# A sketched attention feeding a feed-forward layer: keys and queries projected as loaded in 64-row tiles, and one written-out task list

## The chip, the cores and the metric

The kernel runs on one core of a Trainium2 chip. The core has five engines, each with its own instruction stream in program order: TensorE (PE in the profile, its weight loads PEld), VectorE (DVE), ScalarE (ACT), GpSimd (POOL) and SyncE (SP, which here only issues DMAs). They wait for each other through semaphores. The metric is the device time of one execution in microseconds, less being better.

## The reference, cut to what matters

```
# q, k, v: (4, 4, 1088, 32) = batch, head, token, dim;  S1, S2: (8, 32)
def phi(x):
    a = einsum('rd,bhsd->bhsr', S1, x)
    b = einsum('rd,bhsd->bhsr', S2, x)
    return einsum('bhsi,bhsj->bhsij', a, b).reshape(..., 64)
q_p, k_p = phi(q), phi(k)
kv  = einsum('bhsf,bhsd->bhfd', k_p, v)
z   = sum(k_p, axis=2)
num = einsum('bhsf,bhfd->bhsd', q_p, kv)
den = einsum('bhsf,bhf->bhs', q_p, z)[..., None] + 1e-06
x   = (num / den).transpose(0, 2, 1, 3).reshape(4352, 128)
h   = x @ w_in                       # w_in: (128, 2048)
out = (h * sigmoid(h)) @ w_out       # w_out: (2048, 128), all inputs and the output float32
```

## The kernel before, in words

The work has two parts: attention, once for each of the four batches, and the feed-forward layer, once for each chunk of tokens. Tokens of a batch are numbered 34 to a partition row when they are loaded (`load_kq`, L89), so a head takes 32 partitions and all four heads fill the 128. `transpose_cols` (L154) turns 32x32 blocks on VectorE, after which partitions hold head and dim and columns hold tokens.

One batch of attention: `project_k` (L203) and `project_q` (L210) multiply the turned keys and queries by S1 and S2 for four heads at a time. The weights WK have 128 rows, and four column tiles of 32 (`tile_position=(0, 32 * c)`) put four groups of tokens on the four partition quarters. `tokens` (L218) turns the result back on VectorE. `outer` (L194) forms the 64 products a_i b_j in bf16, for keys into `kp` and for queries into `qp`. `sum_kv` (L234) multiplies `kp` by V over 18 matmuls. The denominator is bilinear in a and b, so `sum_z` (L221) sums the 8x8 products of the keys, `query_weights` (L227) multiplies them by S2, and `mask_weights` (L230) makes of that a third weight WQb for the queries; `denominators` (L252) finishes it with a product, a reduction and a reciprocal, and `divide` (L259) scales the first query features. `turn` (L263) transposes `qp` on TensorE with an identity, a copy takes it out of PSUM, `numerators` (L274) multiplies by the block-diagonal KVbd, and another copy writes `xT`, the feed-forward's input with dims on partitions.

The feed-forward (`Chunk`, L305; `feed_forward`, L346) takes chunks of 256, 512 and 320 tokens for the first batch and then 512 each, 192 at the end. `hidden` (L317) computes two matmuls of up to 512 columns into one of two PSUM tiles (pool `psH`) and one Silu activation of up to 1024 columns on ScalarE; `output` (L329) accumulates with w_out into one PSUM bank. `store` (L291) writes the turned result with four DMAs or more.

What sets the order: the program order is the schedule (`manual_schedule`, L61). The first batch's attention is written out by hand from L436. The attention of later batches is a generator (L364) that the feed-forward's loop advances by one piece for each step (L509 to L515): batch 1 begins at step 5, batch 2 at step 19, batch 3 at step 35. Loads are ordered by dependencies (L138 to L142): each K or Q of a later batch waits for an earlier load, and V of a later batch, which is cast to bf16 on its way and issued by POOL, waits for the load before it. On POOL these loads are the last instructions.

Of the kernel before, what the change touches and what calls it, by code (L numbers as in the profile page):

```python
# [13 lines left out]
AX = mybir.AxisListType  # L14

# [8 lines left out]
def kernel(  # L24
# [13 lines left out]

    B, H, S, D = q.shape
    R = S1.shape[0]  # L40
    HR = H * R
# [7 lines left out]
    YA = 24  # L49
    assert DM == P and HR == 32 and S == 32 * NY and 3 * NC < NY <= 4 * NC  # L50
# [3 lines left out]
    moeg = ctx.enter_context(tc.tile_pool(name="moeg", bufs=8))  # L54
    outb = ctx.enter_context(tc.tile_pool(name="outb", bufs=2))
    psH = ctx.enter_context(tc.tile_pool(name="psH", bufs=2, space=bass.MemoryType.PSUM))
    psO = ctx.enter_context(tc.tile_pool(name="psO", bufs=1, space=bass.MemoryType.PSUM))
    psP = ctx.enter_context(tc.tile_pool(name="psP", bufs=2, space=bass.MemoryType.PSUM))
    psA = ctx.enter_context(tc.tile_pool(name="psA", bufs=1, space=bass.MemoryType.PSUM))

# [7 lines left out]
    QT = [const.tile([P, 4 * NC * 32], FP32, name=f"QT{i}") for i in range(2)]  # L68
    PQ = [const.tile([P, 3, NC, HR], FP32, name=f"PQ{i}") for i in range(2)]
    AW = [const.tile([P, NC * H, R + 1], FP32, name=f"AW{i}") for i in range(2)]  # L70
    WQb = [const.tile([P, HR], FP32, name=f"WQb{b}") for b in range(B)]
    KVbd = [const.tile([P, 2, 2 * D], BF16, name=f"KVbd{b}") for b in range(B)]
# [3 lines left out]
    xT = const.tile([P, NTOK], BF16, name="xT")  # L76

    S12 = const.tile([R, 2, D], FP32, name="S12")  # L80
# [32 lines left out]

    warm = const.tile([P, 1], FP32, name="warm")
    nc.gpsimd.memset(warm, 0.0)
    ident32 = const.tile([32, 32], FP32, name="ident32")
    make_identity(nc, ident32)
    hmask = const.tile([P, H, R], FP32, name="hmask")
    nc.gpsimd.memset(hmask, 0.0)
    for h in range(H):  # L120
        nc.gpsimd.memset(hmask[D * h: D * (h + 1), h, :], 1.0)
    nc.gpsimd.memset(KT[0][:, NY * 32:], 0.0)
    nc.gpsimd.memset(QT[0][:, NY * 32:], 0.0)
    nc.gpsimd.memset(Vx[96:P, :, NY - 3 * NC: NC, :], 0.0)
    nc.gpsimd.memset(KVbd[0], 0.0)
    for i in range(2):
        nc.gpsimd.memset(AW[i][:, :, R:], 1e-6)
    ident_bf = const.tile([P, P], BF16, name="ident_bf")
    make_identity(nc, ident_bf)
    nc.gpsimd.memset(KT[1][:, NY * 32:], 0.0)  # L130
    nc.gpsimd.memset(QT[1][:, NY * 32:], 0.0)
    for b in range(1, B):
        nc.gpsimd.memset(KVbd[b], 0.0)
# [11 lines left out]
    REP32 = const.tile([32, 4, 32], FP32, name="REP32")  # L145
    nc.vector.tensor_copy(out=REP32, in_=bcast(ident32[:, :], 1, 4))
    rep32 = REP32.rearrange("p h d -> p (h d)")
    REPJ = const.tile([R, 4, R], FP32, name="REPJ")
    nc.vector.tensor_copy(out=REPJ, in_=bcast(ident32[:R, :R], 1, 4))
    hm = const.tile([HR, H], FP32, name="hm")  # L150
    nc.vector.tensor_reduce(out=hm, in_=ident32.rearrange("p (h j) -> p h j", h=H),
                            axis=AX.X, op=ALU.add)

    def transpose_cols(dst, src, b, c0, c1):  # L154
        nc.vector.transpose(out=dst[:, c0:c1],  # L155
                            in_=src[b].rearrange("p a d -> p (a d)")[:, c0:c1])


    st_ps = psA.tile([P, 2 * R], FP32, name="st_ps", tag="acc")
    nc.tensor.transpose(st_ps[:D, 0:R], S12[:, 0, :], ident32[:R, :R])  # L160
    nc.tensor.transpose(st_ps[:D, R:2 * R], S12[:, 1, :], ident32[:R, :R])
    ST_sb = const.tile([D, 2 * R], FP32, name="ST_sb")
    nc.vector.tensor_copy(out=ST_sb, in_=st_ps[:D, :])
    rep_ps = psP.tile([P, 2 * R], FP32, name="rep_ps", tag="proj")
    nc.tensor.matmul(rep_ps, rep32, ST_sb, start=True, stop=True)
    s2_ps = psA.tile([HR, D], FP32, name="s2_ps", tag="acc")
    nc.tensor.matmul(s2_ps, REPJ.rearrange("p h j -> p (h j)"), S12[:, 1, :],
                     start=True, stop=True)
    transpose_cols(KT[0], Kx, 0, 0, 2 * NC * 32)
    WK = const.tile([P, 2, H, R], FP32, name="WK")  # L170
    for i in range(2):
        nc.vector.tensor_tensor(out=WK[:, i], in0=bcast(rep_ps[:, i * R: (i + 1) * R], 1, H),  # L172
                                in1=hmask, op=ALU.mult)
    wk = [WK[:, i].rearrange("p h i -> p (h i)") for i in range(2)]
    transpose_cols(KT[0], Kx, 0, 2 * NC * 32, S)


    L1 = const.tile([HR, H, D], FP32, name="L1")
    nc.vector.tensor_tensor(out=L1, in0=bcast(s2_ps[:, :], 1, H), in1=bcast(hm[:, :], 2, D),
                            op=ALU.mult)  # L180
    l4_ps = psA.tile([P, P], FP32, name="l4_ps", tag="acc")
    L4 = const.tile([P, P], FP32, name="L4")

    def l4():
        nc.tensor.matmul(l4_ps, rep32, L1.rearrange("p h d -> p (h d)"), start=True, stop=True)  # L185
        nc.scalar.activation(out=L4, in_=l4_ps, func=ACT.Copy)  # L186

# [6 lines left out]
    def outer(dst, a, bb):  # L194
        nc.vector.tensor_tensor(  # L195
            out=dst.rearrange("p n h i j -> p (n h) i j"),
            in0=bcast(a.rearrange("p n (h i) -> p (n h) i", h=H), 3, R),
            in1=bcast(bb.rearrange("p n (h j) -> p (n h) j", h=H), 2, R), op=ALU.mult)

    def project_k(ps, kt, n0, n1, weights=wk):  # L203
        for i, w in enumerate(weights):
            for c in range(4):
                nc.tensor.matmul(ps[32 * c: 32 * (c + 1), i, :], w,  # L206
                                 kt[:, (c * NC + n0) * 32: (c * NC + n1) * 32],
                                 start=True, stop=True, tile_position=(0, 32 * c))

    def project_q(ps, weights, qt, n0, n1):  # L210
        q4 = qt.rearrange("p (n c x) -> p n c x", c=4, x=32)
        for i, w in enumerate(weights):
            for c in range(4):
                nc.tensor.matmul(ps[32 * c: 32 * (c + 1), i, :].rearrange(  # L214
                                     "p (n x) -> p n x", x=32), w, q4[:, n0:n1, c, :],
                                 start=True, stop=True, tile_position=(0, 32 * c))

    def tokens(dst, ps):  # L218
        nc.vector.transpose(out=dst, in_=ps.rearrange("p a (n r) -> p a n r", r=32))  # L219

    def sum_z(zacc, pk, n0, n1):  # L221
        for n in range(n0, n1):
            s = n % 4
            nc.tensor.matmul(zacc[32 * s: 32 * (s + 1), :], pk[:, 1, n, :], pk[:, 0, n, :],
                             start=(n < 4), stop=(n + 4 >= NC), tile_position=(0, 32 * s))

    def query_weights(m_ps, zt):  # L227
        nc.tensor.matmul(m_ps, L4, zt, start=True, stop=True)

    def mask_weights(b, m_ps):  # L230
        nc.vector.tensor_tensor(out=WQb[b], in0=m_ps,
                                in1=hmask.rearrange("p h i -> p (h i)"), op=ALU.mult)

    def sum_kv(kv_ps, kp, vb):  # L234
        for p in range(2):
            for n in range(NC):
                nc.tensor.matmul(kv_ps[:, p, :],
                                 kp[:, n, 2 * p: 2 * p + 2].rearrange("p h i j -> p (h i j)"),
                                 vb[:, 2 * p: 2 * p + 2, n, :],
                                 start=(n == 0), stop=(n == NC - 1))  # L240

    def keep_kv(copy, b, kv_ps):
        for i in range(2):
            copy(KVbd[b][64 * i: 64 * (i + 1), :, D * i: D * (i + 1)],
                 kv_ps[64 * i: 64 * (i + 1), :, D * i: D * (i + 1)])
# [300 lines left out]
```

## Time and profile before

| | |
|---|---|
| time, median of 3 runs | 123.84 us (123.51 to 124.39) |
| profiled execution: span from first to last instruction | 122.1 us |
| mean granted TensorE clock in it | 0.983 |
| Silu activations (L325) | 72, 67.7 us busy |
| first-layer matmuls (L322), second-layer matmuls (L335) | 41.5 and 39.3 us busy |
| first Silu starts at | 19.18 us |
| last matmul ends, last output turn (L341) starts | 117.45 us, 117.49 us |

The time is what the runs measure; of the profiled execution the page gives its span, which counts from the first to the last instruction and is the clock of all views. Matmul records overlap, so the sum of their durations is more than the time they take; a chain of waits counts each moment once. In a line of a time line the first number is the start and the second the duration, both in us; the bracket at the end is the idle time before the instruction and what ended it. "x4" means four instructions merged.

### The profile page before, as it was taken

To read this page: it belongs to the slowest core of one execution; us is meant where nothing else is said; L and a number is where in the kernel's file an instruction comes from. 1 tells how busy PE (TensorE), PEld (TensorE's weight loads), DVE (VectorE), ACT (ScalarE), POOL (GpSimd) and SP (SyncE) were. 2 spreads that over 40 slices of the span, in tenths; PEclk is the share of its full clock that TensorE was granted. 3 is DMA by queue.
4 is the path that set the end of the run, shared out by engine and by line. 5 is a ranking of instruction groups with operands and counts; after the bars stand their busy time and mean duration, and the time that the engine had idled before them with its cause. 6 is when DMAs were issued, how large, how long until landed. Compare 5 with 4: busy or idle time off the path is not lost.

```text
span 122.1 us, 2269 instructions
## 1 busy us (share of the span) xinstructions
PE 97.7 (80%) x884; PEld 50.5 (41%) x896; DVE 68.7 (56%) x126; ACT 74.2 (61%) x83; POOL 11.8 (10%) x41
## 2 busy tenths in 40 slices
PE   0397849969999649899982999999838989989940
PEld 0265627644445435435432244445304434434630
DVE  1367693499945996993369649953398430020210
ACT  4005466666576725466981379667843899999920
POOL 6604510701600000000000000000000000000000
PEclk9999999999999999999999599999999999999998
DMA  2799997691994500030013000500031005013151
GB/s 52 263 222 319 182 358 127 195 205 62 222 173 109 87 2 0 2 57 0 3 21 65 0 0 5 86 0 5 0 59 27 0 0 86 0 21 53 17 94 27
DMA packets 24314, 9.80 MB, mean 80 GB/s; under 512 B 21104, under 2 KB 22896, under 8 KB 24304
## 3 DMA queue, kind: packets, MB, share of 16 engines
q1 hardware_dynamic: 20352, 8.03, 26.0%
q0 software_dynamic: 3792, 1.36, 9.8%
q10 hardware_dynamic: 160, 0.26, 0.6%
q8 instruction: 7, 0.11, 0.4%
q14 instruction: 3, 0.02, 0.1%
HBM read 8.78 MB, written 2.23 MB: 90 GB/s over the span
## 4 chain that ended last, share of the span: by engine, by line
PE 59%; DVE 22%; ACT 7%; DMA 5%; issue 4%; SPq 0%; DVEq 0%; ACTq 0%
PE h_ps L322 20%; PE o_ps L335 17%; DVE qp L195 7%; ACT g L325 5%; PE qpt_ps L268 4%; PE pq_ps L214 3%; PE num_ps L277 3%; PE pk_ps L206 3%; DMA Kx<-in_k_dram 3%; DVE o_tt L341 3%; PE h_ps L206 2%; DVE PQ L219 2%; DVE qpt L189 2%; DVE den L256 2%; DVE AW L254 2%
## 5 line engine op out<-in xcount | busy, mean ns | idle before, releaser
L325 ACT ACTIVATE g<-h_ps 128x1024 bf16<-128x1024 f32 (+2 forms) x72 | 67.7, 980 | 31.1 <-PE h_ps L322 25.5
L322 PE MATMUL h_ps<-xT,w_in_bf 128*128 128x512 bf16 (+3 forms) x151 | 41.5, 365 | 1.9 <-ACT g L325 1.4
L335 PE MATMUL o_ps<-g,w_out_bf 128*128 128x512 bf16 (+3 forms) x157 | 39.3, 349 | 0.5
L335 PEld LDWEIGHTS <-w_out_bf 128*128 128x128 bf16 x160 | 15.5, 98 | 14.8 <-issue 1.1
L322 PEld LDWEIGHTS <-w_in_bf 128*128 128x128 bf16 x160 | 13.1, 103 | 15.9 <-issue 11.1
L341 DVE STREAM_TRANSPOSE o_tt<-o_ps 128x512 f32<-128x512 f32 (+3 forms) x10 | 6.3, 631 | 20.6 <-PE o_ps L335 18.8
L268 PE MATMUL qpt_ps<-ident_bf,qp 128*128 128x128 bf16 (+1 forms) x72 | 6.7, 235 | 9.2 <-DVE qp L195 8.5
L195 DVE TENSOR_TENSOR kp<-pk 128x1280 bf16<-128x1280 f32 (+1 forms) x8 | 10.8, 1352 | 0.2
L195 DVE TENSOR_TENSOR qp<-aqs,PQ 128x1024 bf16<-128x1024 f32 (+3 forms) x9 | 10.8, 1223 | 0.2
L268 PEld LDWEIGHTS <-qp 128*128 128x128 bf16 (+1 forms) x72 | 5.0, 106 | 12.8 <-DVE qp L195 10.0
L189 DVE COPY qpt<-qpt_ps 128x1024 bf16<-128x1024 bf16 (+2 forms) x11 | 5.9, 540 | 5.7 <-PE qpt_ps L268 5.7
L189 DVE CAST xT<-num_ps 128x512 bf16<-128x512 f32 (+2 forms) x11 | 5.8, 531 | 4.8 <-PE num_ps L277 4.8
L83 POOL DMA_DIRECT2D Vb<-in_v_dram x12 | 6.5, 548 | 15.1 <-DMA Qx<-in_q_dram 12.3
L155 DVE STREAM_TRANSPOSE KT<-Kx 128x1088 f32<-128x1088 f32 (+2 forms) x5 | 5.4, 1075 | 2.1 <-DMA Kx<-in_k_dram 2.1
L277 PE MATMUL num_ps<-qpt,KVbd 128*64 128x512 bf16 (+3 forms) x24 | 4.7, 383 | 2.2 <-DVE qpt L189 1.4
L155 DVE STREAM_TRANSPOSE QT<-Qx 128x512 f32<-128x512 f32 (+3 forms) x8 | 5.7, 718 | 0.0
L277 PEld LDWEIGHTS <-KVbd 128*64 128x64 bf16 x24 | 1.9, 111 | 7.0 <-issue 6.9
L214 PE MATMUL pq_ps<-QT,WK 128*32 128x128 f32 (+2 forms) x112 | 4.7, 284 | 0.0
L206 PE MATMUL h_ps<-KT,WK 128*32 128x160 f32 (+1 forms) x32 | 2.8, 448 | 2.1 <-DVE WK L172 2.1
L206 PE MATMUL pk_ps<-KT,WK 128*32 128x160 f32 (+1 forms) x96 | 4.2, 292 | 0.1
L186 ACT ACTIVATE L<-l_ps 128x128 f32<-128x128 f32 x1 | 0.3, 277 | 6.3 <-PE l_ps L185 6.3
L219 DVE STREAM_TRANSPOSE PQ<-pq_ps 128x256 f32<-128x256 f32 (+2 forms) x7 | 3.3, 470 | 1.0 <-PE pq_ps L214 1.0
(73 smaller groups left out, 61.6 us busy)
## 6 DMA issues: line engine op xcount, KB each, us to landing
Kx<-in_k_dram SPq DMA_DIRECT2D x3, 544.0 KB, 4.8
Qx<-in_q_dram SPq DMA_DIRECT2D x3, 544.0 KB, 6.1
out_dram<-o_tt SPq DMA_DIRECT2D x20, 64.0 KB, 1.9
w_in_f<-in_moe_w_in_dram SPq DMA_DIRECT2D x2, 512.0 KB, 6.1
Vb<-in_v_dram POOLq DMA_DIRECT2D x9, 72.0 KB, 3.8
w_out_bf<-in_moe_w_out_dram POOLq DMA_DIRECT2D x1, 512.0 KB, 8.2
Vx<-in_v_dram SPq DMA_DIRECT2D x3, 144.0 KB, 2.8
Qx<-in_q_dram SPq DMA_DIRECT2D x1, 384.0 KB, 4.9
```

The lines of the kernel that those rows point to most:

```text
L83: ins = eng.dma_start(dst, src)
L155: nc.vector.transpose(out=dst[:, c0:c1], in_=src[b].rearrange("p a d -> p (a d)")[:, c0:c1])
L189: nc.vector.tensor_copy(out=out_, in_=in_)
L195: nc.vector.tensor_tensor(out=dst.rearrange("p n h i j -> p (n h) i j"), in0=bcast(a.rearrange("p n (h i) -> p (n h) i", h=H), 3, R), in1= ...
L206: nc.tensor.matmul(ps[32 * c: 32 * (c + 1), i, :], w, kt[:, (c * NC + n0) * 32: (c * NC + n1) * 32], start=True, stop=True, tile_position= ...
L214: nc.tensor.matmul(ps[32 * c: 32 * (c + 1), i, :].rearrange("p (n x) -> p n x", x=32), w, q4[:, n0:n1, c, :], start=True, stop=True, tile_ ...
L268: nc.tensor.transpose(qpt_ps[:, p, (n - n0) * P: (n - n0) * P + np_], qp[:np_, n, 2 * p: 2 * p + 2].rearrange("p h i j -> p (h i j)"), ide ...
L277: nc.tensor.matmul(num_ps[64 * p: 64 * (p + 1), :ncol], KVbd[b][:, p, :], qpt[:, p, :ncol], start=True, stop=True, tile_position=(0, 64 * p))
L322: nc.tensor.matmul(h[:, i, :self.ntok], w_in_bf[:, j * P: (j + 1) * P], xT[:, self.t0: self.t0 + self.ntok], start=True, stop=True)
L325: nc.scalar.activation(out=self.view(g)[:, :, :self.ntok], in_=h[:, :, :self.ntok], func=ACT.Silu)
L335: nc.tensor.matmul(self.o_ps[:, :self.ntok], w_out_bf[:, j, :], self.view(self.gs[s])[:, i, :self.ntok], start=(j == 0), stop=(j == NJ - 1))
L341: nc.vector.transpose(out=o_tt[:, :self.ntok], in_=self.o_ps[:, :self.ntok])
```

## The change

Three things change together.

The layouts. WK becomes a weight for two heads (64 rows) and both sketches, so `pk` projects keys in 64-row by 32-column tiles, `tile_position=(64 * r, 32 * c)`, with heads 0, 1 in the upper row half and 2, 3 in the lower. The queries get one weight WQ of 32 columns for each head: S1's and S2's columns (constant) and the eight that come from z; `pq` projects all three in one go in 64x64 tiles. Pairs of bf16 query products are turned 32x32 on VectorE as if they were fp32 (`pt`), so TensorE's transposes, the identity and the copies out of PSUM go away, and `nm` multiplies even and odd elements separately in 64x64 tiles, accumulating the two. z is summed from Gram matmuls of the whole feature rows (`zs`). The S weights are turned on VectorE; `wq_const` writes the constant columns of WQ for all four batches on GpSimd.

The order. Each step is a function, and the list ORDER says in which order they are emitted. "zeros n" emits n matmuls of zeros into an unused bank. Letters at the end name an engine for a copy (A, V) or a PSUM tile of the pool `psH` (H). The feed-forward's steps are `f1` (first layer), `sl` (Silu), `f2` (second layer) and `ot` (turn and store); chunks are now 256, 384, 448, then 512 each and 192.

The loads. The early loads lose their dependencies and take another order, all on SP, with the rest of the first batch's queries behind w_in; K and Q of batches 1 to 3 form one chain, each waiting for the one before. Pools: `moeg` 10 instead of 8, `outb` 3 instead of 2, `psP` 1 instead of 2.

```diff
+ORDER = """
+weights, kt 0 0 18, zeros 28, pk 0 0 2 H, weights2, kt 0 18 34
+vc0 2 4, qt 0 0 8, vc0 0 2, zeros 6, pk 0 2 4, tk 0
+kp 0 1 1, zeros 13, zs 0, kp 0 0 0, zc 0 A, kp 0 0 1
+wic 1, wq_const, wic 0, zeros 10, mm 0, mk 0
+wic 2, zeros 6, pq 0 0 4, kp 0 1 0, zeros 4, kv 0
+tq 0 0 4, dn 0 0 4, wic 3, qt 0 8 34, zeros 22, pq 0 4 10 H
+qo 0 0 4, pt 0 0 4, pq 0 10 17, kw_act 0, zeros 3, nm 0 0 4 H
+xc 0 0 4 A, tq 0 4 10, zeros 10, f1 0 0, sl 0 0, f1 0 1
+kt 1 0 34, dn 0 4 10, zeros 10, f1 0 3, sl 0 1, sl 0 3
+tq 0 10 17, f2 0 0, qo 0 4 10, f1 0 2, pt 0 4 10, sl 0 2
+pk 1, dn 0 10 17, nm 0 4 10 H, tk 1, xc 0 4 10 A, kt 2 0 34
...
+sl 2 5, qt 2 0 34, f2 2 2, f2 2 3, f1 3 1, qo 1 8 17
+f2 2 4, f1 3 0, f2 2 5, sl 3 1, f2 2 6, f1 3 6
...
+ot 8, f2 9 0, f2 9 1, sl 9 3, f2 9 2, f2 9 3
+ot 9
+"""
...
-    nc.scalar.dma_start(S12[:, 0, :], S1)
-    nc.sync.dma_start(S12[:, 1, :], S2)
-    k0a = load_kq(nc.sync, 0, k, Kx, 0, 2 * NC)
-    k0b = load_kq(nc.scalar, 0, k, Kx, 2 * NC, NY)
-    q0a = load_kq(nc.sync, 0, q, Qx, 0, YA)
-    v0 = load_v(nc.sync, 0, Vx, k0a)
-    wi0 = begin(nc.sync, w_in_f[:, :half], moe_w_in[:, :half], q0a)
-    wi1 = begin(nc.sync, w_in_f[:, half:], moe_w_in[:, half:])
-    q0b = load_kq(nc.sync, 0, q, Qx, YA, NY, v0)
+    load_kq(nc.sync, 0, k, Kx, 0, 18)
+    sketch(nc.scalar, 0, S1)
+    sketch(nc.scalar, 1, S2)
+    load_kq(nc.sync, 0, k, Kx, 18, NY)
+    load_kq(nc.sync, 0, q, Qx, 0, 8)
+    load_v(nc.sync, 0, Vx)
+    wi = []
+    for i in range(4):
+        wi.append(begin(nc.sync, w_in_f[:, i * CH:(i + 1) * CH], moe_w_in[:, i * CH:(i + 1) * CH]))
+    q0b = load_kq(nc.sync, 0, q, Qx, 8, NY)
...
-    wo = begin(nc.gpsimd, w_out_bf, moe_w_out.rearrange("(j p) m -> p j m", p=P), v0)
-    prev = wi1
+    wo = begin(nc.gpsimd, w_out_bf, moe_w_out.rearrange("(j p) m -> p j m", p=P), wi[1])
+    prev = q0b
     for b in range(1, B):
         load_v(nc.gpsimd, b, Vb[b], prev)
         kb = load_kq(nc.sync, b, k, Kx, after=prev)
-        prev = load_kq(nc.sync, b, q, Qx, after=q0b if b == 1 else kb)
+        prev = load_kq(nc.sync, b, q, Qx, after=kb)
...
+    def zeros(n, ncol=P):
+        if "zps" not in t:
+            t["zps"] = psO.tile([P, CH], FP32, name="zps", tag="ot")
+        for _ in range(n):
+            nc.tensor.matmul(t["zps"][:, :ncol], zw, zw[:, :ncol], start=True, stop=True)
...
+    def wq_const():
+        for b in range(B):
+            nc.gpsimd.tensor_copy(out=WQ[b][:, :, 0:R].rearrange("p h (i e) -> p h e i", e=2),
+                                  in_=WK[:, :, 0, :].rearrange("p h (e i) -> p h e i", e=2))
+            nc.gpsimd.tensor_copy(out=WQ[b][:, :, R: 2 * R], in_=WK[:, :, 1, :])
...
+        for c in range(c0, c1):
+            for r in range(2):
+                rs = slice(64 * r, 64 * (r + 1))
+                nc.tensor.matmul(t["pk_ps", b][32 * c: 32 * (c + 1), r, :NC * 32], w[rs, :],
+                                 KT[b % 2][rs, c * NC * 32: (c + 1) * NC * 32],
+                                 start=True, stop=True, tile_position=(64 * r, 32 * c))
...
+        for g in range(2):
+            for r in range(2):
+                rs = slice(64 * r, 64 * (r + 1))
+                nc.tensor.matmul(t["pq_ps", b, p0][64 * g: 64 * (g + 1), r, :cols].rearrange(
+                                     "p (y x) -> p y x", x=32), w[rs, :], qv[rs, g, p0:p1, :],
+                                 start=True, stop=True, tile_position=(64 * r, 64 * g))
...
+    def pt(b, p0, p1):
+        src = t["qp", b][:, p0:p1].rearrange("p y r j i -> p y r (j i)").bitcast(FP32)
+        dst = t["qT", b][:, :, p0 * 32: p1 * 32, :].rearrange("p r c e -> p r (c e)").bitcast(FP32)
+        nc.vector.transpose(out=dst.rearrange("p r (y x) -> p y r x", x=32), in_=src)
...
+        for e in range(2):
+            for g in range(2):
+                for r in range(2):
+                    gs = slice(64 * g, 64 * (g + 1))
+                    nc.tensor.matmul(t["nm", b, p0][64 * r: 64 * (r + 1), g, :cols],
+                                     KVw[b][gs, e ^ g, r].rearrange("p h d -> p (h d)"),
+                                     t["qT", b][gs, r, p0 * 32: p1 * 32, e],
+                                     start=(e == 0), stop=(e == 1), tile_position=(64 * g, 64 * r))
```

The other steps are named by what they do: `weights` and `weights2` make WK and the S2 weight on VectorE; `kt` and `qt` turn loaded keys and queries; `tk` and `tq` turn projected ones back; `kp` forms a quarter of the key products, `qo` the query products; `mm` and `mk` make the z columns of WQ; `kv`, `kw` (`kw_act` for batch 0) sum and mask the key-value weights; `dn` is the denominator and the division; `xc` writes `xT`; `vc0` and `wic` cast V and w_in to bf16 on ScalarE. An argument list such as "0 4 10" is the batch and a range of the 17 query pieces of 64 tokens.

More of the change, by code (lines that the diff above doesn't have):

```diff
@@ L115, with sketch @@
-    nc.gpsimd.memset(warm, 0.0)
[L116 to L123, printed above, removed]
+    def sketch(eng, i, src):
+        return eng.dma_start(T12[:, i, :], AP(tensor=src.tensor, offset=src.offset,
+                                              ap=[[0, P // R], [D, R], [1, D]]))
@@ L171 @@
[L171 to L181, printed above, removed]
@@ L210, in project_q @@
[L210 to L219, printed above, removed]
@@ L221, in sum_z @@
[L221 to L232, printed above, removed]
@@ new lines, in zc, with mm, mk @@
+    def zc(b, copy):
+        t["zt", b] = work.tile([P, 2 * R], FP32, name="zt", tag="zt")
+        copy(t["zt", b], t["z", b])
+    def mm(b):
+        t["m", b] = psA.tile([P, 2 * R], FP32, name="m_ps", tag="ac")
+        nc.tensor.matmul(t["m", b], L4.rearrange("p h d -> p (h d)"), t["zt", b], start=True, stop=True)
+    def mk(b):
+        nc.vector.tensor_tensor(
+            out=WQ[b][:, :, 2 * R: 3 * R].rearrange("p h (i e) -> p h e i", e=2),
+            in0=t["m", b].rearrange("p (h e i) -> p h e i", h=2, e=2),
+            in1=bcast(bcast(hm2, 2, 2), 3, 4), op=ALU.mult)
@@ new lines, in sl, with f2 @@
+    def sl(c, s):
+        g = moeg.tile([P, 2, CH], BF16, name="g", tag="g")
+        gv, per = view(g, c)
+        nc.scalar.activation(out=gv, in_=t.pop(("h", c, s)), func=ACT.Silu)
+        gt[c, s] = gv
+    def f2(c, s):
+        t0, ntok = CHUNKS[c]
+        if s == 0:
+            op[c] = psO.tile([P, CH], FP32, name="o_ps", tag="ot")
+        g = gt.pop((c, s))
+        per = g.shape[1]
+        for i in range(per):
+            j = per * s + i
+            nc.tensor.matmul(op[c][:, :ntok], w_out_bf[:, j, :], g[:, i, :],
+                             start=(j == 0), stop=(j == NJ - 1))
@@ L292, in store, with ot @@
+    def ot(c):
+        t0, ntok = CHUNKS[c]
+        o_tt = outb.tile([P, CH], FP32, name="o_tt", tag="ott")
+        nc.vector.transpose(out=o_tt[:, :ntok], in_=op[c][:, :ntok])
         for r in range(4):
@@ new lines @@
+    named = {"A": acopy, "V": vcopy}
+    tasks = dict(zeros=zeros, weights=weights, weights2=weights2, wq_const=wq_const, kt=kt, pk=pk,
+                 tk=tk, kp=kp, zs=zs, zc=zc, mm=mm, mk=mk, kv=kv, kw=kw, kw_act=kw_act, qt=qt,
+                 pq=pq, tq=tq, dn=dn, qo=qo, pt=pt, nm=nm, xc=xc, f1=f1, sl=sl, f2=f2, ot=ot,
+                 wic=wic, vc0=vc0)
+    for line in ORDER.strip().splitlines():
+        for entry in line.split(","):
+            what, *args = entry.split()
+            kw_args = {}
+            if args and args[-1] == "H":
+                args.pop()
+                kw_args["ps"] = psH.tile([P, 2, CH], FP32, name="h_ps", tag="h")
+            tasks[what](*[named[x] if x in named else int(x) for x in args], **kw_args)
```

504 lines of the change are left out of this document (203 added, 301 removed).

## The prediction, made before the changed kernel ran

> **What bounds the kernel now.** I read the page's head first, then the stretches by engine, then the chain of waits, and last the time lines of POOL, SP and DVE, because the diff puts new work behind POOL's loads.
>
> ```profile
> PE 97.7 (80%) x884; PEld 50.5 (41%) x896; DVE 68.7 (56%) x126; ACT 74.2 (61%) x83; POOL 11.8 (10%) x41
> PE   0397849969999649899982999999838989989940
> DVE  1367693499945996993369649953398430020210
> ACT  4005466666576725466981379667843899999920
> ```
>
> ```profile
> 40.00:50.00 10.00, 6.51 (x49) 3.80 (x48) 8.63 (x13) 5.18 (x7) 0.00 (x0) 1.00 0.16 27
> 60.00:70.00 10.00, 7.32 (x37) 2.67 (x37) 6.75 (x11) 4.90 (x5) 0.00 (x0) 0.84 0.15 26
> 95.00:110.00 15.00, 14.26 (x71) 6.02 (x71) 3.27 (x6) 14.02 (x15) 0.00 (x0) 1.00 0.13 22
> ```
>
> The bound changes. Up to 19 us the first batch's attention feeds nothing. Around 40 to 50 and 60 to 70 TensorE waits for the next batch's query products on VectorE (2.7 us idle at 66.38). At 95 to 110 the feed-forward runs alone, and PE and ACT are both full (14.26 and 14.02 of 15 us).
>
> ```profile
> 11.64 0.19 DVE L231 TENSOR_TENSOR WQb<-m_ps,hmask 128x32 f32<-128x32 f32 x1 [0.64 <-PE m_ps L228]
> 19.18 1.94 ACT L325 ACTIVATE g<-h_ps 128x1024 bf16<-128x1024 f32 x2 [1.10 <-PE h_ps L322]
> ```
>
> ```profile
> 21.34 0.33 SPq L83 DMA_DIRECT2D Kx<-in_k_dram  x1
> 25.05 0.33 SPq L83 DMA_DIRECT2D Qx<-in_q_dram  x1
> 29.67 0.33 SPq L83 DMA_DIRECT2D Kx<-in_k_dram  x1
> ```
>
> ```profile
> 13.65 2.16 POOL L83 DMA_DIRECT2D Vb<-in_v_dram  x4 [2.82 <-DMA w_in_f<-in_moe_w_in_dram]
> 21.61 2.14 POOL L83 DMA_DIRECT2D Vb<-in_v_dram  x4 [5.80 <-DMA Qx<-in_q_dram]
> 30.21 2.17 POOL L83 DMA_DIRECT2D Vb<-in_v_dram  x4 [6.46 <-DMA Qx<-in_q_dram]
> ```
>
> The query weights are ready at 11.83 and the first Silu starts 7.35 us later. SP's lines show the load chain: each load waits for the one before, so 25.05 - 21.34 = 3.71 us for a K and 29.67 - 25.05 = 4.62 us for a Q. POOL stands between its V loads until that chain releases them; it is done with the last at 32.38. Nothing stands behind them now.
>
> **The step that decides.** The new `wq_const` writes the constant columns of WQ with eight POOL copies, two for each batch. In program order they stand behind all of POOL's DMA issues: w_out, four for batch 1, four for batch 2, four for batch 3. Batch 3's wait for batch 2's queries. `pq 0 0 4`, the first query projection, reads WQ0. Behind it on PE stand `kv 0`, every numerator and the whole feed-forward; DVE stands at `tq 0 0 4` with all later turns behind it, ACT at `kw_act 0` with all Silus. SP is not held.
>
> When is WQ0 written? Batch 0's last query load (416 KB) is now behind w_in on SP. Before, all these loads were in between 13.36 (K1 issued after w_in) and 13.79 (Q1 issued after the last query part). The same bytes, with fewer waits between issues: 12.4 us, bounds 11.0 and 13.8. Then K1, Q1, K2, Q2 one behind another (before, K1 and Q1 ran side by side, 13.36 to 21.34): 4.5 + 4.4 + 3.71 + 4.62 = 17.2, where the first two are estimates between the rows because V1 and w_out run beside them; bounds 4 x 3.71 = 14.8 and 4 x 4.62 = 18.5. Then POOL's reaction (30.21 - 29.67 = 0.54), four issues (2.17) and two copies. No row has a POOL copy; the nearest are its memsets, 0.10 to 0.31 each, so 0.3 for two (bounds 0.2 and 0.6). WQ0: 12.4 + 17.2 + 0.54 + 2.17 + 0.3 = 32.6; bounds 28.7 and 35.6.
>
> Everything ahead of that point I cost at nothing: the new load order, sketches turned on DVE instead of PE, the first key projection, z, `kp`, four w_in copies, 63 idle matmuls ("zeros"). Their counterparts end by about 15 us now, so some 18 us of waiting cover them; in the first rival the cover is gone.
>
> **From WQ0 to the third feed-forward chunk's start (VectorE paces).** Prices are start-to-start in dense stretches of DVE's time line: transpose of 1088 1.22 (48.08 to 49.30), the two outer products of 2304 together 2.55 (42.35 to 44.90), 512 out of PSUM 0.64 (38.43 to 39.07), the four steps of a denominator with 36 heads 1.92 (40.43 to 42.35), with 8 heads 1.09 (14.10 to 15.19); sizes between are interpolated. In DVE's order up to `xc 1 0 8`: batch 0's three pieces (tq, dn, qt, qo, pt) 10.1; three early turns of K and Q 3.7; two `tk` 1.5; batch 1 (mk 0.1, four `kp` of 576 each 2.7, tq 1.4, dn 2.6, kw 0.65, qo 1.15, pt 0.65, xc 0.6) 9.9; two `ot` and a zc 1.0. Sum 26.1. Before it `pq` cold, 0.8 (eight 128-column fp32 instructions took 1.08 at 12.11); in between 1.2 until `pq 0 4 10` passes 22 zeros, and 1.5 for hand-overs. 29.6 us. Bounds: 26.9 with no waits, and 32 with DVE's mean durations (1.30, 1.23 + 1.48, 0.72) in place of start-to-start.
>
> ACT needs less: 4 x 0.91 + 8 x 0.69 + 8 x 0.80 = 15.6 from its first Silu, at about 32.6 + 8.0 = 40.6.
>
> **From there to the last matmul (TensorE paces).** First-layer columns left: 3264 tokens x 16; second layer 3656 x 16. A 512-column pair takes 0.43 in the chain, so 6920 x 16 / 512 x 0.2156 = 46.6. The attention left: batch 1 half a numerator; batch 2 pq, kv, nm; batch 3 all. New shapes: `pk`, eight 64x32 tiles of 288 columns; `pq`, two times four 64x64 tiles; `nm`, two times eight 64x64. None has a row. Nearest: pw_ps, four 128x32 tiles of 288, 0.62 in the chain. Best: all tiles of a group side by side: pk 0.62, pq 1.24, nm 0.5. Row halves one after another: 1.24, 2.48, 1.2. I take the middle (0.9, 1.5, 0.8). z is 18 matmuls, 0.88 (nine took 0.44); kv 0.53; m 0.30. Sum 0.4 + 2.83 + 4.91 = 8.1; bounds 6.6 and 11.4. Waits: PE idled 5% at 95 to 110, so 2.7. Total 46.6 + 8.1 + 2.7 = 57.4. DVE's own list ends at 61.6 + 0.8 + about 6 after WQ0, and the 12.5 us of matmuls behind its last `xc` end before that, so DVE does not bind here.
>
> What the change removes, per batch: 18 PE transposes (1.06 us of chain), project and numerator matmuls from 3.9 to about 3.2. PE's work per batch falls from about 6.2 to 4.9, DVE's stays at 16 to 17 (qpt copies out, `pt` in). This, and stalls like 66.38's, is the gain: 91.7 us from WQ0 to the end against 110.3 from 11.83 before.
>
> **Tail.** Last matmul end to span end: 122.1 - 117.45 = 4.65. The third output buffer takes away 1.76 us ahead of the last o_tt; that is not in my sum.
>
> Sum: 32.6 + 29.6 + 57.4 + 4.65 = 124.3 of span, against 122.1. The page gives no time beyond the span; the median of 123.84 is 1.74 above it, so 126.0.
>
> A row and a rule: at 18.13 eight 256-column matmuls took 1.87 us, at 22.86 0.87, so PE had two speeds, though the granted clock reads 1.00 in both stretches; from WQ0 I price the first 5 us at the slow one. The Trainium skill ("TensorE: Matmul & The Clock Gate", Part 1) has a half-rate clock until about 3.4 us of sustained work; this trace agrees in the ratio, but its first 12 busy us (5.89 to 18.13, with gaps) did not lift it. By the rule the sum is as above; by the row the first chunk is slow too, 2 us more.
>
> **Rivals.**
> First, the copies do not wait: POOL runs them when WK is ready. Then WQ0 comes at 12 and the time is 126.0 - 20.6 = 105.4. For: no row shows a compute instruction behind a waiting load. Against: POOL's loads themselves stay in order, 12.3 us idle for Qx. The Trainium skill ("PSUM — Partial Sum Buffer", Engine vs sequencer instructions) calls GpSimd's queue strict FIFO; by that this rival falls.
> Second, not slower: the load chain is quick, each load 3.71 and the first in at 11, so WQ0 at 28.8 and the time 122.2. It decides below 30.4 (123.84). For: loads are chained with less beside them. Against: Q2 took 4.62 with the same neighbours.
> Third: the 64-row tiles do not run side by side. A 288-column fp32 tile alone lies between 0.42 (pw_ps's mean) and 0.62, say 0.49: pk 3.9, pq 3.9, nm 16 x 0.12 = 1.9 per batch, 18.6 instead of 8.1: 136.5. Against: four column tiles now take 0.62, not four times a 0.42 record. The Trainium skill (same TensorE page, Part 3) lets row and column tiles run together; that is my best end.
>
> **Chances.** Forecast 0.62, alone 120 to 131; first 0.09, second 0.22, third 0.07. About 1% (122.6 to 125.1) is what a measurement here can tell. Of the forecast 0.15 lies below, 0.27 within; of the second 0.6 and 0.35. Faster 0.09 + 0.13 + 0.09 = 0.31; same 0.08 + 0.17 = 0.25; slower 0.44. The range, 118 to 132, leaves out the first and third and a little more.
>
> **What the profile would show.** Right: POOL idle before its copies, released by the Qx load, copies near 32; PE, DVE and ACT nearly empty from about 14 to 32; first Silu near 40; then PE over 90% busy. Wrong: copies near 12 (first rival); PE waiting for DVE after 65; pk far from 0.9.

## The result, and the profile after

The changed kernel takes 122.44 us (median of 20 runs, 120.38 to 123.34), the kernel before 124.12 us beside it (20 runs, 122.46 to 125.52). The ratio is 0.984, 95% interval 0.980 to 0.988. The ratios here leave disturbed runs out, but three of the profiles shown further down (of the kernels of 110.46, 121.42 and 122.64 us) are of executions 1.1 to 1.7 us above their medians. So it is 1.6% faster where the likeliest case said 1.7% slower. The profiled execution took 121.77 us with a span of 119.1 us.

The head of the page of the changed kernel: busy time of each engine, then tenths in 40 slices, here 2.98 us each.

```profile
PE 88.3 (74%) x857; PEld 48.1 (40%) x864; DVE 67.6 (57%) x128; ACT 73.3 (62%) x91; POOL 12.1 (10%) x47
PE   6499000000089999999999999999999999999920
DVE  0349300000048999999999999799398973020210
ACT  2217300000004779969879988999989789999800
PEclk9999975555558999999999999999999999999999
```

TensorE's busy time fell from 97.7 to 88.3 us. There is a hole of about seven slices (13 to 33 us) in which TensorE, VectorE and ScalarE do nothing, and from then on TensorE is full. The time lines of GpSimd and TensorE show what ends the hole (start, duration, engine, line, operation, and in brackets the idle time before it and its releaser):

```profile
12.59 2.16 POOL L157 DMA_DIRECT2D Vb<-in_v_dram  x4 [1.38 <-DMA Qx<-in_q_dram]
22.66 2.15 POOL L157 DMA_DIRECT2D Vb<-in_v_dram  x4 [7.91 <-DMA Qx<-in_q_dram]
30.71 2.15 POOL L157 DMA_DIRECT2D Vb<-in_v_dram  x4 [5.90 <-DMA Qx<-in_q_dram]
32.90 0.20 POOL L251 COPY WQ<-WK 128x16 f32<-128x16 f32 x1
33.03 0.20 POOL L253 COPY WQ<-WK 128x16 f32<-128x16 f32 x1
...
33.28 0.70 PE L352 MATMUL pq_ps<-QT,WQ 64*64 64x128 f32 x8 [21.57 <-POOL WQ L253]
```

The copies of 16 columns each follow the last V load directly, 0.14 us apart, and the first query projection starts after the second of them, 21.57 us idle. The waits view puts numbers on who stood (engine and line, releaser: us in total, times, longest):

```profile
DVE PQ L358 <- PE pq_ps L352: 23.0, 2, 21.2
ACT KVw L335 <- PE kv_ps L316: 22.7, 1, 22.7
...
PE pq_ps L352 <- POOL WQ L253: 21.6, 1, 21.6
```

The three waits are one and the same stretch, passed on from engine to engine. SyncE's time line shows the load chain that sets its length:

```profile
12.30 0.33 SPq L157 DMA_DIRECT2D Kx<-in_k_dram  x1
19.10 0.33 SPq L157 DMA_DIRECT2D Qx<-in_q_dram  x1
22.44 0.33 SPq L157 DMA_DIRECT2D Kx<-in_k_dram  x1
26.04 0.33 SPq L157 DMA_DIRECT2D Qx<-in_q_dram  x1
30.17 0.33 SPq L157 DMA_DIRECT2D Kx<-in_k_dram  x1
```

Last, busy time by stretch (stretch, its length, then PE, PEld, DVE, ACT, POOL busy, the granted clock, DMA share, GB/s). The first two lie in the hole; the third goes from the first query projection to the end of `xc 1 0 8`, the fourth from there to the last matmul.

```profile
20.00:25.00 5.00, 0.00 (x0) 0.00 (x0) 0.00 (x0) 0.00 (x0) 2.15 (x4) 0.50 0.61 209
25.00:30.00 5.00, 0.00 (x0) 0.00 (x0) 0.00 (x0) 0.00 (x0) 0.00 (x0) 0.50 0.82 181
33.28:59.90 26.62, 26.07 (x353) 16.82 (x354) 24.65 (x52) 19.54 (x30) 0.78 (x6) 0.94 0.22 44
59.90:113.91 54.01, 53.42 (x388) 25.09 (x393) 36.53 (x64) 48.74 (x53) 0.00 (x0) 1.00 0.18 32
```

TensorE is busy in 26.07 of 26.62 and in 53.42 of 54.01 us. VectorE, which the prediction took for the pace of the third stretch, has 24.65 of 26.62.

### The profile page after: what moved, and what is told of

Its sections match the earlier page's. It is cut to its first block, busy times and chain, and to the rows that moved or that the text cites. A ratio compares the mean times of both kernels' runs of the same rounds, so it can differ in the third digit from the quotient of the medians.

```text
span 119.1 us, 2189 instructions
## 1 busy us (share of the span) xinstructions
PE 88.3 (74%) x857; PEld 48.1 (40%) x864; DVE 67.6 (57%) x128; ACT 73.3 (62%) x91; POOL 12.1 (10%) x47
## 3 DMA queue, kind: packets, MB, share of 16 engines
q1 hardware_dynamic: 20768, 8.29, 26.9%
## 4 chain that ended last, share of the span: by engine, by line
PE 42%; DMA 23%; DVE 17%; ACT 8%; issue 2%; SPq 2%; POOL 2%; POOLq 0%; ACTq 0%; DVEq 0%
PE o_ps L437 18%; PE h_ps L419 16%; DMA Qx<-in_q_dram 11%; DMA Kx<-in_k_dram 9%; ACT g L426 8%; DVE qp L378 3%; DMA T<-in_S_dram 3%; DVE kp L284 2%; DVE PQ L358 2%; PE zps L236 2%; DVE KT L258 2%; SPq L157 2%; POOL Vb L157 2%; PE pq_ps L352 2%; DVE qT L384 1%
## 5 line engine op out<-in xcount | busy, mean ns | idle before, releaser
L419 PE MATMUL h_ps<-xT,w_in_bf 128*128 128x512 bf16 (+4 forms) x156 | 39.8, 347 | 0.5
L437 PE MATMUL o_ps<-g,w_out_bf 128*128 128x512 bf16 (+4 forms) x157 | 37.5, 346 | 0.4
L352 PE MATMUL pq_ps<-QT,WQ 64*64 64x288 f32 (+3 forms) x48 | 4.0, 409 | 21.6 <-POOL WQ L253 21.6
L443 DVE STREAM_TRANSPOSE o_tt<-o_ps 128x512 f32<-128x512 f32 (+4 forms) x10 | 6.3, 635 | 13.9 <-PE o_ps L437 13.8
L236 PE MATMUL zps<-zw 128*128 128x128 bf16 x112 | 10.7, 264 | 1.1 <-POOL hm L196 1.1
L284 DVE TENSOR_TENSOR kp<-pk 128x576 bf16<-128x576 f32 x16 | 11.3, 740 | 0.0
L236 PEld LDWEIGHTS <-zw 128*128 128x128 bf16 x112 | 9.0, 123 | 3.7 <-issue 2.5
L378 DVE TENSOR_TENSOR qp<-PQ 128x1024 bf16<-128x1024 f32 (+4 forms) x9 | 10.3, 1146 | 0.1
L384 DVE STREAM_TRANSPOSE qT<-qp 128x512 f32<-128x512 f32 (+4 forms) x9 | 5.9, 659 | 0.1
L341 DVE STREAM_TRANSPOSE QT<-Qx 128x1088 f32<-128x1088 f32 (+2 forms) x5 | 5.3, 1057 | 0.0
```

Of the source, the lines that this page charges most:

```text
L236: nc.tensor.matmul(t["zps"][:, :ncol], zw, zw[:, :ncol], start=True, stop=True)
L284: nc.vector.tensor_tensor(out=o, in0=bcast(s[:, :, 0, 4 * e: 4 * e + 4], 2, R), in1=bcast(s[:, :, 1], 3, 4), op=ALU.mult)
L352: nc.tensor.matmul(t["pq_ps", b, p0][64 * g: 64 * (g + 1), r, :cols].rearrange("p (y x) -> p y x", x=32), w[rs, :], qv[rs, g, p0:p1, :], s ...
L378: nc.vector.tensor_tensor(out=t["qp", b][:, p0:p1].rearrange("p y r j i -> p (y r) j i"), in0=bcast(fa, 2, R), in1=bcast(fb, 3, R), op=ALU ...
L384: nc.vector.transpose(out=dst.rearrange("p r (y x) -> p y r x", x=32), in_=src)
L419: nc.tensor.matmul(h[:, i, :], w_in_bf[:, j * P: (j + 1) * P], xT[:, t0: t0 + ntok], start=True, stop=True)
```

## The experiments

Each kernel was timed beside the kernel before on the same chip, in three rounds, or in five where less was expected. Ratios are to the kernel before; kernels sent at different times are compared by ratio.

**The hold itself.** Theory A: GpSimd's copies stand behind its V loads, and all the time of the hole is on the path. Rivals: the hole covers work that takes its place when it is gone; or the copies are late for another reason. Three kernels end the hold in three ways.

First, the copies are emitted ahead of GpSimd's loads:

```
-weights, kt 0 0 18, zeros 28, ...
-wic 1, wq_const, wic 0, ...
+kt 0 0 18, zeros 28, ...
+wic 1, wic 0, ...
...
+    weights()
+    wq_const()
     wo = begin(nc.gpsimd, w_out_bf, ...)
     prev = q0b
     for b in range(1, B):
         load_v(nc.gpsimd, b, Vb[b], prev)
```

> The changed kernel with one thing undone: the eight GpSimd copies of wq_const (and the two VectorE steps that make WK) are emitted ahead of GpSimd's load issues instead of behind them. Theory A, the place in GpSimd's queue holds everything back one for one: the copies run near 6 us, the first query projection starts near 11.7 (where PE stood waiting in the changed kernel, 33.28 - 21.57), and the time falls by 21.6 less what the loads then cost. K of batch 1 landed at 19.1 and is now wanted near 17, so 2 to 3 us come back: 103 us, 101 to 105. Rival B, the hold hides a wait for loads that was there anyway (K1, Q1, K2 and Q2 landed at 19.1, 22.4, 26.0 and 30.2): most of it comes back and the time stays above 112.

Measured: 103.16 us, ratio 0.834 (0.831 to 0.837). From GpSimd's time line:

```profile
5.68 0.20 POOL L244 COPY WQ<-WK 128x16 f32<-128x16 f32 x1 [1.33 <-DVE WK L234]
...
10.13 1.29 POOL L157 DMA_DIRECT2D w_out_bf<-in_moe_w_out_dram  x1 [3.22 <-DMA w_in_f<-in_moe_w_in_dram]
12.45 2.16 POOL L157 DMA_DIRECT2D Vb<-in_v_dram  x4 [1.03 <-DMA Qx<-in_q_dram]
22.96 2.15 POOL L157 DMA_DIRECT2D Vb<-in_v_dram  x4 [8.36 <-DMA Qx<-in_q_dram]
```

The copies now wait 1.33 us for their input and for nothing else. The loads keep their times, as they hang on each other. The first query projection starts at 12.02 us, 21.3 us sooner, and the time falls by 18.6 us (0.984 - 0.834 of 123.8). The difference lies in the stage from there to the end of `xc 1 0 8`, 29.95 us (to 41.97) against 26.62 in the changed kernel. In it VectorE now waits for the load of batch 1's keys:

```profile
19.41 1.31 DVE L260 STREAM_TRANSPOSE KT<-Kx 128x1088 f32<-128x1088 f32 x1 [2.87 <-DMA Kx<-in_k_dram]
```

Second, the copies stay where they are in the list, on VectorE (`nc.gpsimd.tensor_copy` becomes `nc.vector.tensor_copy` in L251 and L253):

> The changed kernel with the eight copies on VectorE instead of GpSimd, at the same place of the list. If it is GpSimd's queue that holds them, the time is that of the kernel with the copies ahead of the loads, plus eight small VectorE instructions of about 0.1 us each ahead of mk 0: 103 to 105. If it is the copies' own cost or the loads that count, the time stays near 122.

Measured: 103.52 us, ratio 0.838 (0.832 to 0.843). The same as the first, so what matters is the queue that the copies stood in, not where the list has them.

Third, a smaller dose. The copies stay behind the loads, but the V loads of batches 2 and 3 no longer wait for the query loads:

```
-        load_v(nc.gpsimd, b, Vb[b], prev)
+        load_v(nc.gpsimd, b, Vb[b], q0b)
```

> The changed kernel with the copies left where they are, but V of batches 2 and 3 waits only for the first batch's queries, as V of batch 1 does, and no longer for later Q loads. GpSimd's twelve issues then take 3 x 2.16 us from 12.6 on, and the copies come near 19.5 to 20.5 instead of 32.9. Theory A: the time falls by as much, 12.5 to 13.5, to about 109.5. Rival B: less than half of that, above 116. If the V loads push K1 and Q1 back, VectorE waits for its first turn of batch 1 and up to 2 us of the gain are lost.

Measured: 110.46 us, ratio 0.891 (0.887 to 0.896). The copies were later than expected. Let go early, the eighth V load waited 1.13 us, by the profile for the load of w_out, and the last four 2.29 us for an earlier V load:

```profile
12.53 3.76 POOL L157 DMA_DIRECT2D Vb<-in_v_dram  x7 [1.02 <-DMA Qx<-in_q_dram]
17.41 0.55 POOL L157 DMA_DIRECT2D Vb<-in_v_dram  x1 [1.13 <-DMA w_out_bf<-in_moe_w_out_dram]
20.25 2.14 POOL L157 DMA_DIRECT2D Vb<-in_v_dram  x4 [2.29 <-DMA Vb<-in_v_dram]
22.44 0.20 POOL L251 COPY WQ<-WK 128x16 f32<-128x16 f32 x1
```

The first copy came 10.5 us sooner (22.44 against 32.90) and the ratio fell by 0.984 - 0.891 = 0.093, some 11.5 us of 123.8. Each microsecond of this part of the hold costs about one of time; no cover takes it up. The whole hold, 21.3 us, costs 15% of the time before, 18.6 us. Without it the change gains 17%.

**The idle matmuls.** The prediction counted the zero matmuls once as 1.2 us of waiting and else as covered. They are left out here; nothing reads them.

```
     def zeros(n, ncol=P):
+        return
```

With the copies ahead of the loads:

> As the kernel with the copies ahead of the loads, and all zero matmuls left out (they write a bank that nobody reads, so nothing computed is missing). Theory C, they hold TensorE at its full speed: without them the first projections and the first chunk's matmuls run at half speed (0.47 in place of 0.22 for a pair of 256 columns), and the time is 1 to 3 us more than with them. Rival D, they only stand in the way (in the changed kernel 22 of them are 1.87 us of the chain): the time is 0 to 2 us less.

Measured: 102.49 us, ratio 0.828 (0.825 to 0.832): 0.7 us below the first kernel, at the edge of what the intervals can tell. With the hold left in place:

> The changed kernel with its multiplier copies still behind the V loads, and without the zero matmuls, which nothing reads. The prediction counted 1.2 us of waiting for the second query group behind 22 zeros; the trace has them at 35.49 to 37.36 us, 1.87 us. Theory A (they only stand in the way): 1.2 to 2.5 us faster than the changed kernel, 120 to 121.2. Theory B (after 21.6 us without work TensorE is slow, and they warm it up beside a wait): same time or slower, 122 to 124, with the first chunks' matmuls longer.

Measured: 121.42 us, ratio 0.984 (0.977 to 0.992). That is the ratio of the changed kernel itself: neither theory's number. The time line of TensorE in this kernel:

```profile
33.30 0.71 PE L353 MATMUL pq_ps<-QT,WQ 64*64 64x128 f32 x8 [21.57 <-POOL WQ L254]
33.94 1.14 PE L317 MATMUL kv_ps<-Vb,kp 128*128 128x64 bf16 x18
36.63 0.92 PE L353 MATMUL h_ps<-QT,WQ 64*64 64x192 f32 x8 [1.54 <-DVE QT L342]
...
38.99 1.87 PE L420 MATMUL h_ps<-xT,w_in_bf 128*128 128x256 bf16 x8 [0.48 <-ACT xT L230]
41.11 1.01 PE L420 MATMUL h_ps<-xT,w_in_bf 128*128 128x256 bf16 x4 [0.26 <-ACT g L427]
```

Where the 22 zeros stood there is now a wait of 1.54 us for a VectorE turn, and the first feed-forward matmuls take 1.87 us for eight, where the changed kernel has 1.04. The kernel of 102.49 us, which has no zeros either, shows the same two: 1.53 and 1.86 us. The cover gone, the other engine is the pace.

**Which engine paces the stage after the hold?** The prediction said VectorE. In this kernel its turns of late queries and of batch 1's keys move into the hold, where it has nothing to do; TensorE's list stays:

```
-tq 0 0 4, dn 0 0 4, wic 3, qt 0 8 34, zeros 22, pq 0 4 10 H
+tq 0 0 4, dn 0 0 4, wic 3, zeros 22, pq 0 4 10 H
-kt 1 0 34, dn 0 4 10, ...
+dn 0 4 10, ...
-wic 2, zeros 6, pq 0 0 4, ...
+wic 2, zeros 6, qt 0 8 34, kt 1 0 34, pq 0 0 4, ...
```

> The changed kernel, its copies still behind the V loads, with two of VectorE's turns (the first batch's late queries, 832 columns, and the second batch's keys, 1088 columns) moved ahead of the first query projection, into the hold in which VectorE has nothing to do. TensorE's instructions and order stay. From 33.28 to 59.90 us the changed kernel's VectorE is busy 24.65 us and TensorE 26.07 of 26.62. Theory A (VectorE's list paces that stage, as the prediction says): 1.04 + 1.27 = 2.3 us off, 120.1 (119.4 to 120.8). Theory B (TensorE paces it): within 0.7 us of the changed kernel's 122.4, and xc 1 0 8 ends again some 26 us after the copies.

Measured: 122.64 us, ratio 0.995 (0.990 to 1.000). Not faster; the interval even lies above that of the changed kernel by a little. One line of VectorE's time line in the changed kernel, and the same step here:

```profile
37.91 0.58 DVE L358 STREAM_TRANSPOSE PQ<-h_ps 128x384 f32<-128x384 f32 x1 [0.31 <-PE h_ps L352]
```

```profile
39.32 0.58 DVE L358 STREAM_TRANSPOSE PQ<-h_ps 128x384 f32<-128x384 f32 x1 [1.95 <-PE h_ps L352]
```

VectorE got there without the two turns and waited 1.95 us, where it had waited 0.31: TensorE was still at its 22 zeros (2.54 us in this execution, 2.06 in the changed kernel's) and the projection behind them. By its time, theory A falls for this cut alone. Then both cuts together, turns in the hold and no zeros:

> The changed kernel, copies behind the V loads, with both edits that alone moved nothing: no zero matmuls (121.42 us alone, ratio to the kernel before 0.9843) and the two VectorE turns moved into the hold (122.64 us alone, 0.995). Theory A (from the copies to the third chunk TensorE and VectorE are each full to within 2 us; a cut on one side leaves the other as the pace): cut together the stage shortens by about 2 us, from 27 to 28 us after the first query projection to 25 or 26, and the time to about 119.5 (118.5 to 120.5; ratio 0.96 to 0.975). Theory B (something third sets the stage, such as ScalarE's copies and Silus, or slow matmuls after the idle stretch): again 121.4 to 122.6, and the stage 27 to 28 us.

Measured: 119.77 us, ratio 0.966 (0.962 to 0.971), as theory A said. The stretch from the first query projection (32.84) to the end of `xc 1 0 8` (58.00):

```profile
32.84:58.00 25.16, 23.37 (x304) 13.78 (x305) 22.77 (x50) 19.54 (x30) 0.77 (x6) 1.00 0.25 48
```

25.16 us against 26.62. TensorE and VectorE pace this stage side by side: neither cut alone made the kernel faster, and the two together gave 1.8% (0.984 to 0.966).

**Do the 64-row tiles run side by side?** The third rival said no. Here the key and query projections have weights of all 128 rows with one half zero, so the two row halves come one after the other; the copies are ahead of the loads and there are no zeros, as in the kernel of 102.49 us. The multipliers are written in two parts instead of one.

```
-            for r in range(2):
-                rs = slice(64 * r, 64 * (r + 1))
-                nc.tensor.matmul(t["pk_ps", b][32 * c: 32 * (c + 1), r, :NC * 32], w[rs, :],
-                                 KT[b % 2][rs, c * NC * 32: (c + 1) * NC * 32], ...
-                                 tile_position=(64 * r, 32 * c))
+        for r in range(2):
+            for c in range(c0, c1):
+                nc.tensor.matmul(t["pk_ps", b][32 * c: 32 * (c + 1), r, :NC * 32], WZ[:, r, :],
+                                 KT[b % 2][:, c * NC * 32: (c + 1) * NC * 32], ...
+                                 tile_position=(0, 32 * c))
```

> The kernel with the copies ahead of the loads and without the zero matmuls (102.49 us), with the key and query projections taken out of their 64-row tiles: weights of 128 rows with one half zero, so that the two row halves come one behind the other where they ran side by side; the columns stay tiled by 32 and 64. Theory A (row tiles run side by side, so that a group costs one stream of 0.42 us per pass and not two): each of 4 key groups goes from 0.70 to about 1.15 us and each of 9 query groups from 0.6 to about 1.0, 5.4 us more of TensorE, some 4.5 of them after 17.6 us where it paces: 107 (105.5 to 108.5). Theory B (the row tiles take turns, the third rival of the prediction): the groups keep their times and the kernel stays within 0.7 us of 102.5. The multipliers' writes are two in place of one, 0.17 us more per batch on VectorE.

Measured: 107.69 us, ratio 0.873 (0.868 to 0.878), 5.2 us more than with 64-row tiles (5.5 by the ratios). One group of key projections with 64-row tiles (the kernel without zeros), and with full rows:

```profile
21.68 0.72 PE L274 MATMUL pk_ps<-KT,WK 64*32 64x288 f32 x16
```

```profile
24.25 1.18 PE L279 MATMUL pk_ps<-KT,WZ 128*32 128x288 f32 x16
```

Same columns, same number of instructions, and each instruction alone has the same median (0.415 and 0.406 us). Only side by side do they take 0.72 us instead of 1.18. The third rival falls.

**Can more be had without the hold?** Two orders of VectorE's list, both on the kernel of 102.49 us. In it VectorE waited for the load of batch 1's keys with batch 0's steps queued behind:

```profile
18.28 1.31 DVE L261 STREAM_TRANSPOSE KT<-Kx 128x1088 f32<-128x1088 f32 x1 [1.48 <-DMA Kx<-in_k_dram]
```

```
-kt 1 0 34, dn 0 4 10, zeros 10, ...
+dn 0 4 10, zeros 10, ...
-pk 1, dn 0 10 17, ...
+kt 1 0 34, pk 1, dn 0 10 17, ...
```

> The kernel with the copies ahead of the loads and without the zero matmuls (102.49 us), with the transpose of the second batch's keys moved from before dn 0 4 10 to before pk 1 in the list. There VectorE waited 1.48 us for the load of the keys and then transposed 1.31 us with the first batch's queries queued behind it. Theory A (TensorE paces from the first chunk on, 17.6 us; between 17.59 and 30 us it is busy 11.30 of 12.41 us): the most to gain is its idle time there, 1.1 us: 101.4 to 102.5. Theory B (VectorE's order sets the end up to the third chunk): the 2.8 us come off nearly whole, about 100 (99.7 to 101).

Measured: 102.75 us, ratio 0.836 (0.829 to 0.843). Then also the late queries' turn behind the first group's features (`qt 0 8 34` and the two `pq` that need it go behind `pt 0 0 4` and `nm 0 0 4`):

> The kernel of the run before last but one in this list (second keys' transpose moved to before pk 1), and also the transpose of the first batch's late queries (1.04 us at 14.14 us) moved behind the first query group's features, so that the first chunk does not wait for it. Theory A (TensorE paces from the first chunk on, so an earlier start is kept): 1.0 us below the kernel with the keys' move alone, first Silu at 17.6 in place of 18.64 us. Theory B (VectorE's stage sets the end of the first batch, and the order inside it is indifferent): the same time within 0.4 us.

Measured: 102.91 us, ratio 0.834 (0.828 to 0.839). Neither is below 0.828, so theory B of the first falls, and of its theory A, which bounds the gain at 1.1 us, a gain of nothing is left. Theory A of the second falls too: its time is that of the first within 0.4 us, as theory B said. In the second the first chunk's input was ready at 15.94 us (`xT` 15.56 + 0.38, against 17.53), and its first Silu still came at 18.68: `pq` stands ahead of `f1` in TensorE's list and waited 0.50 us for the turn that had been moved. A wait changed its place.

Last, zeros only where TensorE waits anyway: 14 ahead of `pq 0 4 10`, 5 ahead of `f1 0 0`:

> The kernel with the copies ahead of the loads (103.16 us with all zero matmuls, 102.49 with none), with 14 zero matmuls ahead of pq 0 4 10 and 5 ahead of f1 0 0 alone: TensorE waits there anyway, 1.69 us for the turned queries and 0.48 for the first chunk. Without zeros the first eight 256-column matmuls took 1.86 us, with all of them 1.04. Theory A (a stretch of work just before makes them quick, and in an idle place it is free): 1.04 to 1.2 us for those eight, 101.4 to 102.2. Theory B (it takes a longer stretch of work, or the gain is lost because TensorE's later work waits for VectorE): eight again in about 1.8, or the time within 0.4 us of 102.49.

Measured: 103.00 us, ratio 0.842 (0.836 to 0.848). The first eight feed-forward matmuls took 1.03 us instead of 1.86, as theory A said, and the time did not follow; the ratio is even above 0.828, by more than the intervals. The 0.8 us came back as waits of TensorE, 0.68 us for a Silu and 1.05 us for VectorE's `PQ` ahead of `pk 1`, so that `pk 1` starts at 21.66 us where it started at 21.68. That is the mechanism of theory B's second half, but the time is not within its 0.4 us: it is 0.5 us more by the medians and 1.6 by the ratios, and what made it longer is not shown. Six kernels without the hold lie between 102.5 and 103.5 us; the first without zeros, 102.49 us, has the lowest median.

## Why the prediction was wrong

Its mechanism was right, and its sign was wrong. The sum gave 124.3 us of span; 119.1 was measured. (The rest: 2.67 us outside the span against 1.74, and the median 0.67 above the profiled run; -5.2 + 0.93 + 0.67 = -3.6 = 122.44 - 126.0, rounded.)

| step | predicted | measured | off |
|---|---|---|---|
| first query projection can start | 32.6 | 33.28 | +0.7 |
| from there to the end of `xc 1 0 8` | 29.6 | 26.6 | -3.0 |
| to the last matmul | 57.4 | 54.0 | -3.4 |
| tail | 4.65 | 5.2 | +0.55 |

The mechanism of "The step that decides" held. The chain began at 12.30 (predicted 12.4), its four loads took 30.17 - 12.30 = 17.9 (17.2), GpSimd's reaction 0.54 (0.54), and the copies came directly behind the four issues. That the sum of the loads came out so near is in part luck: the first, which lay beside w_out and V1, took 6.8 us, far over the estimate of 4.5, and the others 3.34, 3.60 and 4.13, each under its price. The Trainium skill ("PSUM — Partial Sum Buffer", Engine vs sequencer instructions) has GpSimd's queue as strict FIFO; this trace agrees, with the copies at 32.90 us behind the loads and at 5.68 us ahead of them. The first rival falls with that. Its price of 105.4 is near what its premise gives when it is made true (103.16), but again with luck: it starts from a forecast that was 3.6 us too high, and it left out that the stage up to `xc 1 0 8` is then 3.3 us longer.

The step that failed first is the sentence "Before it `pq` cold, 0.8 ...; in between 1.2 until `pq 0 4 10` passes 22 zeros, and 1.5 for hand-overs". VectorE's list itself was well priced: from its first turn (34.05) to the end of `xc 1 0 8` it is 25.85 us, predicted 26.1. But those prices were start-to-start, so the hand-overs were in them already, and adding 1.5 counted them twice. The 1.2 us behind the zeros was 0.31, because VectorE did its own 1.04 us turn and 1.10 us of products and turns at the same time. 26.1 + 0.8 alone would have been 26.9, the lower bound, and 26.6 came. "VectorE paces" was half of the truth: the stage has two engines that are full, which the experiment with both cuts shows.

The step that failed second is "I take the middle (0.9, 1.5, 0.8)", and beside it "z is 18 matmuls, 0.88" and the waits of 5%. Three groups of the changed kernel, each with the line behind it:

```profile
63.29 0.66 PE L352 MATMUL pq_ps<-QT,WQ 64*64 64x256 f32 x8
63.88 0.60 PE L419 MATMUL h_ps<-xT,w_in_bf 128*128 128x512 bf16 x2
...
65.71 0.45 PE L393 MATMUL num_ps<-qT,KVw 64*64 64x288 bf16 x8
66.09 0.60 PE L419 MATMUL h_ps<-xT,w_in_bf 128*128 128x512 bf16 x2
...
67.49 0.72 PE L271 MATMUL pk_ps<-KT,WK 64*32 64x288 f32 x16
68.14 0.39 PE L419 MATMUL h_ps<-xT,w_in_bf 128*128 128x512 bf16 x1
```

From the start of a group to the start of the next, a `pk` takes 0.65 us, a half `pq` 0.53 to 0.59, a half `nm` 0.34 to 0.38, z 0.44. For `pk` and `pq` these are the side-by-side prices (0.62 and 1.24 whole). `nm`, 0.72 whole, is near the middle of 0.8 and not at its best price of 0.5. The nearest row, four column tiles in 0.62, had already spoken for them, and so did the rule of the Trainium skill ("TensorE: Matmul & The Clock Gate", Part 3) that row and column tiles run together; the runs agree, 0.72 against 1.18 us. For `pk` and `pq` the middle was chosen between a likely and an unlikely value and belonged to neither.

The trace divides the 54.0 us into 45.5 for the feed-forward, by the prediction's own price for a column, 6.4 for the attention's groups and 2.1 for waits and hand-overs; the sum had 46.6, 8.1 and 2.7. The feed-forward is 1.1 us less because six second-layer matmuls of the third chunk ran while VectorE still finished `xc 1 0 8`. TensorE itself idled only 0.6 of the 54.0 us (54.01 - 53.42): the 5% was read off the kernel before at 95 to 110 us (14.26 busy of 15), where the changed kernel has 14.89.

The second rival's time, 122.2, is near the result, but its mechanism, a load chain done by 28.8, is not what happened. The tail is 0.55 us longer than before. The trace places this at the last four stores: SyncE starts them 0.38 us after the last turn ends, where before it was 0.03, and takes 2.07 us to issue them, where before it took 1.78. Why was not tested. One reading of the prediction was off without touching its sum: the 2.7 us idle at 66.38 is TensorE's weight load; the matmuls waited 2.38.

The error in sign came from the 3.0 and 3.4 us of these two stages, both on one side and most of them surcharges on top of measured prices, in a forecast whose distance to no change was 2 us.

What stays open: why moving VectorE's turns alone seems to cost 1% (0.995 against 0.984). In its profiled execution TensorE was slow for longer after the hold (the 22 zeros 2.54 us against 2.06, the next two query groups 0.92 and 0.95 against 0.56 each); whether that holds in its other runs was not seen.

## What to carry to other kernels

When instructions change engine, read the new engine's queue from the top: here eight copies of 0.2 us, placed behind loads that wait for other loads, cost 19 us and hid nearly the whole of a 17% gain. A price taken start-to-start in a dense stretch has the hand-overs in it; add a wait only where a named instruction is late. Where two engines are both full in a stage, cutting one shows nothing, so test both cuts together before calling either harmless.

## What the runs showed of the hardware

The granted clock and TensorE's real speed are two things. The changed kernel's clock row shows 0.50 in the hold. The kernel with the hold and without zeros shows 1.00 in the same stretch, with TensorE as idle:

```profile
PEclk9999999999999999999999999999999999999998
```

Yet in that kernel the first eight 256-column matmuls took 1.87 us, 1.8 times the 1.04 us that the changed kernel has after its zeros. So the row does not tell how fast the next matmuls are.

Which speed they have goes by the work just before: 1.03 us for the eight where TensorE had worked for 4 to 5 us nearly without a gap (14 and 5 zeros; or both cuts together, from 32.85 to 37.33 us), 1.86 and 1.87 where a gap of about 1.5 us lay in that stretch. How much work it takes is not fixed. In the kernel of 102.49 us the eight began at 17.59, and from 21.15 us on, 3.6 us later, TensorE is at full speed. In that of 102.75 us, with the same list of TensorE, they began at 17.63, and at 22.40, 4.8 us later, `pk 1` still took 1.21 us instead of 0.72. The Trainium skill ("TensorE: Matmul & The Clock Gate", Part 1) has the full rate after about 3.4 us of sustained work; these runs agree that it takes sustained work, but 3.6 us of it was enough in one kernel and 4.8 us not in another.

A V load issued from GpSimd can wait for an earlier V load: with the loads let go early the last four waited 2.29 us, by the one profile of that kernel for one before them. With the 1.13 us of the eighth, this moved the copies from the 19.5 to 20.5 us expected to 22.44.
